# A fused RWKV-5 attention and cosine-router MoE kernel: drains on GpSimd, a branch hint, two loads swapped and two small tables moved

## The chip, the cores and the metric

The kernel runs on one core of a Trainium2 chip. The core has a matrix engine (TensorE, PE in the profile, with its weight loads as PEld), a vector engine (VectorE, DVE), an activation engine (ScalarE, ACT), a programmable engine (GpSimd, POOL) and an engine that mostly issues transfers (SyncE, SP). Each engine runs its own list of instructions in order, and they wait for one another by semaphores. The metric is the time on the device for one execution, in microseconds; a lower time is better. A profiled execution gives the trace that all views below are taken from.

## The reference, cut to what matters

Two computations follow each other. The first is a recurrence over 768 steps for 4 batches of 8 heads of 48 columns; the second sends each of the 3072 resulting rows to one of 8 experts.

```python
# attention: r, k, v are (4, 8, 768, 48); w and u are (8, 48)
for t in range(S):
    kt, vt, rt = k[:, :, t], v[:, :, t], r[:, :, t]
    cur = einsum('bhd,bhe->bhde', u[None] * kt, vt)
    y[:, :, t] = einsum('bhd,bhde->bhe', rt, state + cur)
    state = w[None, :, :, None] * state + einsum('bhd,bhe->bhde', kt, vt)
# x = y as 3072 rows of 384
logits = normed(x) @ normed(expert_emb).T / tau
expert_idx = argmax(logits); gate_w = softmax(logits)[expert_idx]
for e in range(8):                       # w1[e] is 384 x 1024, w2[e] is 1024 x 384
    h = maximum(x[mask] @ w1[e], 0.0)
    out[mask] = gate_w[mask, None] * (h @ w2[e])
```

All data are float32.

## The kernel before

**The attention** is cut into 24 units: 6 chunks of 128 steps by 4 batches. Unit i needs a K, an R and a V tile of 192 KB each; `load` issues the three, and the units are pipelined, five units ahead for the loads. For each unit GpSimd makes three products of 128x384: K times a power of the decay (`scaled`), K times u (`own_k`), and that times R (`own_r`). The last of them gives each step's own term, which VectorE sums to `diag` and ScalarE multiplies with V (`own_rows`).

```python
def load(k, i, K=None):
    ...
    nc.sync.dma_start(out=K, in_=of(k.k))
    R = k.Rpad[i % len(k.Rpad)]
    nc.sync.dma_start(out=R[:, :, 0:D], in_=of(k.r))
    V = k.io.tile([128, H, D], F32, name="V", tag="V")
    if i == 0:
        k.u_bc = ...                      # u, broadcast over the partitions
        nc.sync.dma_start(out=k.u_bc..., in_=...)
    nc.sync.dma_start(out=V, in_=of(k.v))
    k.loaded[i] = (K, R, V)

def scaled(k, i):
    k.nc.gpsimd.tensor_mul(k.Kpad[i % len(k.Kpad)][:, :, 0:D], k.loaded[i][0], k.kpow)
def own(k, i):
    own_k(k, i)
    own_r(k, i)
def own_k(k, i):
    k.KU[i] = ...
    k.nc.gpsimd.tensor_mul(k.KU[i], k.loaded[i][0], k.u_bc)
def own_r(k, i):
    k.nc.gpsimd.tensor_mul(k.KU[i], k.KU[i], k.loaded[i][1][:, :, 0:D])
```

`build_first` loads units 0 to 3 and calls `own_k(k, 0)`; the first turn of the loop (i = -1) then calls `scaled` for unit 1, `own_r` for unit 0 and `own` for unit 1, in this order.

**The tables** are small constants that the routing needs. `build_turned` is a generator: each `next(tables)` emits the VectorE instructions up to the next `yield`. The first three steps come in turns 1, 2 and 3, the last one in turn 9 (2 * B + 1 with B = 4).

```python
def build_turned(k):
    ...                                   # bits of a partition number, `own`, `mask`
    yield
    nc.vector.scalar_tensor_tensor(k.turned, k.qt, own[:, 1:2], k.turned, ALU.is_equal, ALU.mult)
    nc.vector.tensor_scalar_add(k.turned, k.turned, -1.0)      # both 128x64
    k.tie = pool.tile([128, E], F32, name="tie")
    nc.vector.tensor_scalar(k.tie, k.number, N + 1.0 / 16, None, ALU.mult)
    yield
```

**The experts** follow the attention, eight turns with the weights loaded ahead. In each turn GpSimd only issues indirect transfers: it gathers rows of x for an expert three turns ahead, and scatters the finished rows of this one to the output. Each of them is one DMA_INDIRECT of 128 rows or fewer; two more gathers stand in the attention's end. TensorE never stops in these turns.

```python
for i in range(E):
    doubled = blocks[i].weigh_out() if i > 0 else blocks[0].halves()
    for b in at(i + 1):
        b.hidden(doubled)
    do(doubled)
    if i == E - 1:
        blocks[i].rest()                  # rows past 256: scatters
    ready = [b.weigh() for b in at(i + 2)] + [b.halves() for b in at(i + 1)]
    blocks[i].out(itertools.chain(*ready))    # the first 256 rows: two scatters
    first_weights(i + 3)
    ...                                   # turn of i + 2, rest() of turns before the last
    for b in at(i + 3):
        b.gather()
    second_weights(i + 2)
```

**The general path** lies behind a branch at the end (`again`). It is for inputs that the quick path can't do (an expert with too many rows, decays out of range); with these inputs it is not entered, and every engine loads a flag and jumps over it.

```python
left = nc.values_load(flag[0:1, 0:1], min_val=0, max_val=1)   # L1458
with tc.If(left > 0):                                         # L1459
    ...                                                       # hundreds of instructions
```

Behind the branch each engine brings its semaphores to the values that the general path would have left, GpSimd does so for those of its own transfers with one INC_SWDGE_SEM, and a closing sequence with drains and barriers of all engines ends the program (L1602 in the profile).

Of the kernel before, what the change touches and what calls it, by code (L numbers as in the profile page):

```python
# [17 lines left out]
B, H, S, D = 4, 8, 768, 48  # L18
DM, E, F = H * D, 8, 1024
# [29 lines left out]
def build_first(k):  # L49


    nc, pool = k.nc, k.aconst
    wc = pool.tile([128, NP], F32, name="wc")
    nc.vector.memset(wc, 1.0)
    with nc.allow_non_contiguous_dma(reason="384 words"):
        for s, q in ((0, nc.sync), (1, nc.scalar)):
            q.dma_start(out=wc[s * DP : s * DP + D, :], in_=k.w.rearrange("(p s) d -> s d p", s=2)[s])
    k.ones = k.const.tile([128, 128], F32, name="ones")
    nc.vector.memset(k.ones, 1.0)
    wide = k.work.tile([128, 512], F32, name="wide", tag="AT1")  # L60
    nc.vector.memset(wide, 1.0)
    k.ident = k.const.tile([128, 128], F32, name="ident")
    make_identity(nc, k.ident)

    def busy(columns):
        ps = k.ps.tile([128, 512], F32, name="wake", tag="y")
        nc.tensor.matmul(ps[:, 0:columns], k.ones, wide[:, 0:columns], start=True, stop=True)

    for _ in range(WAKE):
        busy(512)  # L70
    k.Kpad, k.Rpad = (
        [pool.tile([128, H, DP], F32, name=f"{name}{i}") for i in range(count)]
        for name, count in (("Kpad", 4), ("Rpad", AHEAD + 2))
    )
    pads = k.Kpad + k.Rpad
    for t in pads:
        nc.gpsimd.memset(t[:, :, D:DP], 0.0)
    load(k, 0, k.Kpad[0])
    for i in range(1, AHEAD - 1):
        load(k, i)  # L80
    load_rows(k)


    nc.gpsimd.tensor_scalar(wc, wc, W_MIN, W_MAX, ALU.max, ALU.min)
    build_numbers(k)
    own_k(k, 0)
    t = pool.tile([128, NP, C], F32, name="wpow")
    for p in range(NP):
        nc.vector.tensor_tensor_scan(
            t[:, p, :], wc[:, p : p + 1].to_broadcast([128, C]), k.ones, 1.0, ALU.mult, ALU.mult  # L90
        )
    mid = pool.tile([128, NP], F32, name="mid")
    nc.vector.reciprocal(mid, t[:, :, C // 2])
    kp = k.work.tile([128, NP, C], F32, name="kp", tag="AT0")
    nc.vector.tensor_mul(kp, t[:, :, ::-1], mid[:, :, None].to_broadcast([128, NP, C]))
    k.rpow = pool.tile([128, NP, C], F32, name="rpow")
    for p in range(NP):
        nc.scalar.mul(k.rpow[:, p, :], t[:, p, :], mid[:, p : p + 1])
    cast(k)

    kt = turned_k(k, 0)
    k.KT[0] = k.work.tile([128, NP, C], F32, name="KT", tag="KT")
    nc.vector.tensor_mul(k.KT[0], kt, kp)
    turn_r(k, 0)
    ps = k.ps.tile([128, NP, 2, DP], F32, name="kpT", tag="xp")
    for p in range(NP):
        nc.tensor.transpose(ps[:, p].rearrange("q s d -> q (s d)"), kp[:, p, :], k.ident)
    busy(192)
    k.kpow = pool.tile([128, H, D], F32, name="kpow")
    nc.vector.tensor_copy(k.kpow.rearrange("q (p s) d -> q p s d", s=2), ps[:, :, :, 0:D])  # L110
    first = k.Kpad[0].rearrange("q (p s) d -> q p s d", s=2)[:, :, :, 0:D]
    nc.vector.tensor_mul(first, first, ps[:, :, :, 0:D])
    k.wC = t[:, :, C - 1 : C].to_broadcast([128, NP, D])
# [77 lines left out]
def build_turned(k):  # L191


    nc, pool = k.nc, k.const
    no_counts(k)
    bits = pool.tile([2 * QS, 3], I32, name="bits")
    nc.vector.tensor_scalar(bits[:, 0:1], k.part, 2, E - 1, ALU.arith_shift_right, ALU.bitwise_and)
    nc.vector.tensor_scalar(bits[:, 1:2], k.part, 3, None, ALU.bitwise_and)
    nc.vector.tensor_scalar(bits[:, 2:3], k.part, 3, 4, ALU.arith_shift_right, ALU.bitwise_and)
    yield  # L200
    own = pool.tile([2 * QS, 3], F32, name="own")
    nc.vector.tensor_copy(own, bits)
    nc.vector.tensor_add(own[:, 1:2], own[:, 1:2], own[:, 2:3])
    yield
    k.mask = pool.tile([2 * QS, E], F32, name="mask")
    nc.vector.tensor_scalar(k.mask, k.number, own[:, 0:1], None, ALU.is_equal)
    yield
    nc.vector.scalar_tensor_tensor(k.turned, k.qt, own[:, 1:2], k.turned, ALU.is_equal, ALU.mult)
    nc.vector.tensor_scalar_add(k.turned, k.turned, -1.0)

    k.tie = pool.tile([128, E], F32, name="tie")
    nc.vector.tensor_scalar(k.tie, k.number, N + 1.0 / 16, None, ALU.mult)
    yield
# [72 lines left out]
def load(k, i, K=None):  # L286

    nc = k.nc
    c, b = divmod(i, B)

    def of(src):
        return src[b, :, c * C : (c + 1) * C, :].rearrange("h s d -> s h d")

    K = k.io.tile([128, H, D], F32, name="K", tag="K") if K is None else K[:, :, 0:D]
    nc.sync.dma_start(out=K, in_=of(k.k))
    R = k.Rpad[i % len(k.Rpad)]
    nc.sync.dma_start(out=R[:, :, 0:D], in_=of(k.r))
    V = k.io.tile([128, H, D], F32, name="V", tag="V")
    if i == 0:
        k.u_bc = k.aconst.tile([128, H, D], F32, name="u_bc")  # L300
        nc.sync.dma_start(
            out=k.u_bc.rearrange("p h d -> p (h d)"),
            in_=bass.AP(tensor=k.u.tensor, offset=k.u.offset, ap=[[0, 128], [1, DM]]),
        )
    nc.sync.dma_start(out=V, in_=of(k.v))
    k.loaded[i] = (K, R, V)


def pair(t, p):
# [7 lines left out]
# [7 lines that stand above are left out]
    k.KU[i] = k.work.tile([128, H, D], F32, name="KU", tag="KU")  # L324
# [5 lines that stand above are left out]
# [8 lines left out]
def own_rows(k, i, half):  # L338
    if half == 0:
        k.xd[i] = k.work.tile([128, H, D], F32, name="xd", tag="xd")  # L340
    diag, V = k.diag[i], k.loaded[i][2]
    for h in range(half * H // 2, (half + 1) * H // 2):
        k.nc.scalar.mul(k.xd[i][:, h, :], V[:, h, :], diag[:, h : h + 1])  # L343

# [499 lines left out]
def attention(k):  # L844
# [16 lines left out]
    emb, tables = build_experts(k), build_turned(k)  # L861
    for i in range(-1, units):
# [16 lines left out]
        if i == B + 3:  # L879
            norms(k, k.groups[0])  # L880
        on(scaled, i + 2)
        if i < 0:
            own_r(k, 0)
        on(own, i + 2)
        for n in SQUARES.get(i, (i - 1,)):
            of_group(squares, n)
# [28 lines left out]
        whole(taken, i - 6, "xp")  # L915
        whole(exps, i - 4)
        on(carry, i)
        if i in (1, 2, 3):
            next(tables)
        whole(summed, i - 6)  # L920
        on(scores, i + 1)
# [16 lines left out]
            build_constants(k)  # L938
        if i in (1, 2, 3):
            next(emb)  # L940
        if i == 2 * B + 1:
            next(tables)
        if 3 <= i < 3 + len(k.ring):
            k.nc.gpsimd.memset(k.ring[i - 3], 0.0)
        if j == 8:
# [426 lines left out]
def experts(k):  # L1372

    blocks = [Block(k, r) for r in TURN]
    for b, (w1, w2) in zip(blocks, k.weights):
        b.w1, b.w2 = w1, w2

    def at(i):
        return [blocks[i]] if i < E else []

    def first_weights(i):
        for b in at(i):
            b.w1 = w1_tile(k)
            load_w1(k, expert_number(k, b.rank), b.w1)

    def second_weights(i):
        for b in at(i):
            b.w2 = w2_tile(k)
            load_w2(k, expert_number(k, b.rank), b.w2)

    for b in blocks[0:2]:
        b.gather()
        b.turn()
    do(blocks[1].Tx)
    do(blocks[1].weigh())
    do(blocks[0].weigh_out())
    blocks[0].plain()
    first_weights(2)
    blocks[2].gather()
# [4 lines that stand above are left out]
        do(doubled)  # L1404
        if i == E - 1:
            blocks[i].rest()
        ready = [b.weigh() for b in at(i + 2)] + [b.halves() for b in at(i + 1)]
        blocks[i].out(itertools.chain(*ready))
        first_weights(i + 3)
        for b in at(i + 2):  # L1410
            b.turn()
            do(b.Tx)
        if 256 < blocks[i].n and i < E - 1:
            blocks[i].rest()
            if i == 2:
                decays(k)
        for b in at(i + 3):
            b.gather()
        second_weights(i + 2)


# [26 lines left out]
def again(k):  # L1448


    nc, tc, need = k.nc, k.tc, k.need
# [4 lines left out]
    nc.vector.tensor_copy(flag[:, 0:1], some)  # L1456
    nc.vector.tensor_copy(flag[:, 1:2], k.far)
    left = nc.values_load(flag[0:1, 0:1], min_val=0, max_val=1)  # L1458
    with tc.If(left > 0):  # L1459
        nc.sync.dma_start(out=k.need_dram.rearrange("e g -> (e g)").unsqueeze(0), in_=as_int(k, need))  # L1460
        far = nc.values_load(flag[0:1, 1:2], min_val=0, max_val=1)
        with tc.If(far > 0):
            no_counts(k)
            recur(k)
            with ExitStack() as ctx:
                attention_pools(k, ctx)
                for c in range(NCH):
# [4 lines left out]
                    out=k.need_dram.rearrange("e g -> (e g)").unsqueeze(0), in_=as_int(k, grouped(k, count))  # L1472
# [134 lines left out]
```

## Time and profile before

The time is 406.03 us (median of 3 runs, 405.99 to 406.11). The profiled execution has a span of 403.8 us.

| stage, us from the span's start | what runs | PE busy in it |
|---|---|---|
| 0 to 131 | attention and routing, 24 units | 22.43 of the first 25, 34.58 of the next 35, 70.01 of the next 71 |
| 131 to 160 | last routing, two early expert tiles | 28.64 of 29 |
| 160 to 385 | eight experts | 225.00 of 225 |
| 385 to 404 | last scatters, branch, closing sequence | 6.73 of 19 |

Over the whole span PE is busy for 387.4 us (96%), VectorE for 254.3 (63%), ScalarE for 172.6 (43%) and GpSimd for 161.1 (40%). Such a table is read by asking for each stage which engine's waits end last. Where PE is full, moving the work of another engine changes nothing unless PE waits for it; where no engine is busy, in the last stage, the time lies in transfers and in instructions that the busy columns leave out. In the group and timeline views a row shows the engine, the line of the source, the operation, the tile written and the tiles read, and the time; a bracket behind a row tells how long the engine stood idle before it and what released it. A "q" behind an engine's name (POOLq) stands for instructions that only its sequencer carries out: branches, semaphore waits, drains.

### The profile page before, as it was taken

To read this page: it belongs to the slowest core of one execution; us is meant where nothing else is said; L and a number is where in the kernel's file an instruction comes from. 1 tells how busy PE (TensorE), PEld (TensorE's weight loads), DVE (VectorE), ACT (ScalarE), POOL (GpSimd) and SP (SyncE) were. 2 spreads that over 40 slices of the span, in tenths; PEclk is the share of its full clock that TensorE was granted. 3 is DMA by queue.
4 is the path that set the end of the run, shared out by engine and by line. 5 is a ranking of instruction groups with operands and counts; after the bars stand their busy time and mean duration, and the time that the engine had idled before them with its cause. 6 is when DMAs were issued, how large, how long until landed. Compare 5 with 4: busy or idle time off the path is not lost.

```text
span 403.8 us, 9257 instructions
## 1 busy us (share of the span) xinstructions
PE 387.4 (96%) x3542; PEld 352.9 (87%) x3542; DVE 254.3 (63%) x601; ACT 172.6 (43%) x523; POOL 161.1 (40%) x216
## 2 busy tenths in 40 slices
PE   7999999999999999999999999999999999999980
PEld 4988888888888877899999999999999999799670
DVE  6886888787788650677668666367267257466210
ACT  3888776777676413333333332232233233232110
POOL 7998795858663242301503202402321330300120
PEclk9999999999999999999999999999999999999995
DMA  8999777767616961246527341613524440420110
GB/s 156 192 221 220 156 155 146 155 137 152 130 41 211 335 233 38 85 159 210 199 67 248 95 157 39 223 41 153 174 83 156 136 140 2 134 82 1 58 40 26
DMA packets 93801, 54.39 MB, mean 135 GB/s; under 512 B 76938, under 2 KB 88381, under 8 KB 93747
## 3 DMA queue, kind: packets, MB, share of 16 engines
q1 hardware_dynamic: 90242, 44.26, 41.3%
q0 software_dynamic: 3296, 9.44, 7.3%
q8 instruction: 30, 0.49, 0.5%
q14 instruction: 25, 0.20, 0.2%
q10 hardware_dynamic: 208, 0.00, 0.0%
HBM read 44.45 MB, written 9.63 MB: 134 GB/s over the span
## 4 chain that ended last, share of the span: by engine, by line
PE 83%; ACT 3%; issue 3%; POOL 3%; DVE 2%; DMA 2%; SPq 1%; POOLq 0%; ACTq 0%
PE ps L1223 25%; PE ps L1287 16%; PE ps L1327 5%; PE at L385 4%; PE y L449 4%; PE ps L1341 4%; PE early_h L1033 3%; PE early_y L1042 3%; PE ps L1201 3%; PE yrows L467 3%; PE ps L1171 2%; PE y L440 2%; PE rt L357 2%; PE kt L366 2%; PE xp L553 2%
## 5 line engine op out<-in xcount | busy, mean ns | idle before, releaser
L1087 POOL DMA_INDIRECT out_dram<-y,to x25 | 30.2, 1206 | 173.5 <-issue 116.7
L1223 PE MATMUL ps<-xTe,w 128*128 128x192 f32 (+3 forms) x336 | 62.9, 327 | 0.0
L1223 PEld LDWEIGHTS ps<-xTe,w 128*128 128x128 f32 x336 | 55.9, 190 | 0.5
L343 ACT ACTIVATE xd<-V,diag 128x48 f32<-128x48 f32 x184 | 46.2, 325 | 0.0
L391 DVE TENSOR_TENSOR AT<-at,umask 128x512 f32<-128x512 f32 x48 | 32.7, 685 | 10.8 <-PE at L385 10.7
L1230 ACT ACTIVATE hT<-hT 128x384 f32<-128x384 f32 (+3 forms) x42 | 22.0, 523 | 32.4 <-DVE hT L1253 19.7
L1287 PE MATMUL ps<-Tw,Sh 128*128 128x192 f32 x192 | 32.5, 326 | 0.0
L1287 PEld LDWEIGHTS ps<-Tw,Sh 128*128 128x128 f32 x192 | 31.4, 190 | 0.0
L1078 POOL DMA_INDIRECT G<-xs,take x25 | 27.0, 1079 | 10.5 <-issue 4.0
L1223 PE MATMUL ps<-Tx,Sw 128*128 128x192 f32 (+3 forms) x168 | 29.6, 326 | 0.0
L385 PE MATMUL at<-RT,KT 48*128 48x128 f32 x384 | 27.9, 285 | 0.2 <-DVE RT L359 0.2
L1223 PEld LDWEIGHTS ps<-Tx,Sw 128*128 128x128 f32 x168 | 27.6, 190 | 0.1
L1240 DVE TENSOR_TENSOR u<-ps,p 128x384 f32<-128x384 f32 (+3 forms) x14 | 7.8, 558 | 31.0 <-ACT p L1237 16.3
L449 PE MATMUL y<-AT,V 128*48 128x128 f32 (+1 forms) x384 | 26.0, 277 | 0.0
L385 PEld LDWEIGHTS at<-RT,KT 48*128 48x128 f32 x384 | 23.3, 187 | 2.5 <-issue 0.9
L329 POOL TENSOR_TENSOR KU<-KU,Rpad 128x384 f32<-128x384 f32 x24 | 24.2, 1007 | 1.8
L314 POOL TENSOR_TENSOR Kpad<-K,kpow 128x384 f32<-128x384 f32 x23 | 23.2, 1008 | 0.9 <-DMA K<-in_k_dram 0.8
L449 PEld LDWEIGHTS y<-AT,V 128*48 128x48 f32 (+1 forms) x384 | 19.9, 124 | 4.1 <-issue 3.8
L1287 PE MATMUL ps<-w,hT 128*128 128x192 f32 x128 | 23.4, 326 | 0.0
L325 POOL TENSOR_TENSOR KU<-K,u_bc 128x384 f32<-128x384 f32 x23 | 23.3, 1012 | 0.0
L555 ACT COPY xT<-xp 128x384 f32<-128x384 f32 x24 | 11.5, 480 | 25.4 <-PE xp L553 25.4
L1250 ACT ACTIVATE hT<-ps 128x384 f32<-128x384 f32 (+3 forms) x14 | 6.9, 491 | 35.7 <-PE ps L1223 35.7
(240 smaller groups left out, 818.5 us busy)
## 6 DMA issues: line engine op xcount, KB each, us to landing
w<-in_moe_w_dram SPq DMA_DIRECT2D x16, 1536.0 KB, 7.4
Rpad<-in_r_dram SPq DMA_DIRECT2D x24, 192.0 KB, 3.9
V<-in_v_dram SPq DMA_DIRECT2D x24, 192.0 KB, 4.2
xs<-X SPq DMA_DIRECT2D x24, 192.0 KB, 2.6
K<-in_k_dram SPq DMA_DIRECT2D x23, 192.0 KB, 3.3
G<-xs,take POOLq DMA_INDIRECT x27, 3.2
out_dram<-y,to POOLq DMA_INDIRECT x25, 3.6
Kpad<-in_k_dram SPq DMA_DIRECT2D x1, 192.0 KB, 3.4
```

What stands on the lines that cost most here:

```text
L314: k.nc.gpsimd.tensor_mul(k.Kpad[i % len(k.Kpad)][:, :, 0:D], k.loaded[i][0], k.kpow)
L325: k.nc.gpsimd.tensor_mul(k.KU[i], k.loaded[i][0], k.u_bc)
L329: k.nc.gpsimd.tensor_mul(k.KU[i], k.KU[i], k.loaded[i][1][:, :, 0:D])
L343: k.nc.scalar.mul(k.xd[i][:, h, :], V[:, h, :], diag[:, h : h + 1])
L385: nc.tensor.matmul(at[s][:, p, :], KT[rows, p, :], RT[rows, p, :], start=True, stop=True)
L391: k.nc.vector.tensor_mul(a, k.at[i][s], k.umask[:, None, :].to_broadcast([128, NP, C]))
L449: mm(y[s][u * DP : u * DP + n, q, :], V[:, h * D : h * D + n], AT[s][:, p, :], start=(c == 0 and q == 0), stop=True, skip_group_check=True,)
L1078: nc.gpsimd.indirect_dma_start(out=G[0:n, :], out_offset=None, in_=k.xs[:, :], in_offset=IndirectOffsetOnAxis(ap=take[0:n], axis=0), bound ...
L1087: put = k.nc.gpsimd.indirect_dma_start(out=k.out[:, :], out_offset=IndirectOffsetOnAxis(ap=to, axis=0), in_=y, in_offset=None, bounds_chec ...
L1223: nc.tensor.matmul(ps[:, j, :], weights[:, (f + j) * 128 : (f + j + 1) * 128], moving, start=(first and j == 0), stop=True, skip_group_che ...
L1230: nc.scalar.activation(h, h, ACT.Relu)
L1287: nc.tensor.matmul(ps, a[:, f, :], b[:, f, :], start=(first and f == 0), stop=(f == NF // 2 - 1), skip_group_check=True)
```

## The change

Four edits, which do not touch each other.

1. **Drains.** A drain instruction is added on GpSimd at the end of each of the experts' turns 0 to 6, behind the gathers, and in turn 7 between the scatters of `rest()` and the two last ones. It has no semaphore to wait for or to set. That makes eight in all. They are meant to let GpSimd settle its transfers while TensorE works.
2. **A hint for the branch.** PE, DVE, ACT and POOL are told that the jump over the general path is likely. The call stands ahead of the experts; in the built program the hint is the first instruction of each of these four engines, behind the opening barrier.
3. **First V behind second K and R.** V of unit 0 is issued after K and R of unit 1, directly ahead of V of unit 1. With it `own_r` of unit 0 moves ahead of `scaled` of unit 1 on GpSimd. No transfer and no product is added.
4. **Tables in turns 1 to 5.** A `yield` between the two 128x64 operations splits the last step in two, and the five steps are taken in turns 1 to 5; nothing is left in turn 9.

```diff
     build_numbers(k)
-    own_k(k, 0)
+    own(k, 0)
@@ build_turned
     nc.vector.scalar_tensor_tensor(k.turned, k.qt, own[:, 1:2], k.turned, ALU.is_equal, ALU.mult)
+    yield
     nc.vector.tensor_scalar_add(k.turned, k.turned, -1.0)
@@ load
     V = k.io.tile([128, H, D], F32, name="V", tag="V")
+    k.loaded[i] = (K, R, V)
     ...
-    nc.sync.dma_start(out=V, in_=of(k.v))
-    k.loaded[i] = (K, R, V)
+    for n in () if i == 0 else (0, 1) if i == 1 else (i,):
+        nc.sync.dma_start(out=k.loaded[n][2], in_=of(k.v, n % B))
@@ attention, in the loop
-        if i < 0:
-            own_r(k, 0)
...
-        if i in (1, 2, 3):
+        if 0 < i < B + 2:
             next(tables)
...
-        if i == 2 * B + 1:
-            next(tables)
@@ experts
+    k.tc.mark_branch_hint_location(
+        "left", "LikelyTaken", engines=[... ("PE", "DVE", "Activation", "Pool")]
+    )
     for b in blocks[0:2]:
...
         if i == E - 1:
             blocks[i].rest()
+            k.nc.gpsimd.drain()
...
         for b in at(i + 3):
             b.gather()
+        if i < E - 1:
+            k.nc.gpsimd.drain()
         second_weights(i + 2)
@@ again
-    with tc.If(left > 0):
+    with tc.If(left > 0, label="left"):
```

More of the change, by code (lines that the diff above doesn't have):

```diff
@@ L289, in load, with of @@
     c, b = divmod(i, B)
-    def of(src):
+    def of(src, b=b):
         return src[b, :, c * C : (c + 1) * C, :].rearrange("h s d -> s h d")
@@ L1389, in second_weights @@
             load_w2(k, expert_number(k, b.rank), b.w2)
+    k.tc.mark_branch_hint_location(
+        "left", "LikelyTaken", engines=[getattr(mybir.EngineType, e) for e in ("PE", "DVE", "Activation", "Pool")]
+    )
     for b in blocks[0:2]:
```

## The prediction

> **What bounds the kernel now.** I read the page first: busy times, then the chain of waits.
>
> ```profile
> PE 387.4 (96%) x3542; PEld 352.9 (87%) x3542; DVE 254.3 (63%) x601; ACT 172.6 (43%) x523; POOL 161.1 (40%) x216
> PE 83%; ACT 3%; issue 3%; POOL 3%; DVE 2%; DMA 2%; SPq 1%; POOLq 0%; ACTq 0%
> ```
>
> PE carries 83% of the chain, and the table by stage shows it full from 160 to 385 us. No part of the change adds or removes a matmul, so in 225 of 404 us nothing can be gained. What is left is the head (0 to 25 us), the attention where VectorE delays PE, and the tail behind 385 us. Each of the four edits aims at one of these. I looked at the tail first, because there all busy columns are almost empty. Its instructions run on the sequencers, so I asked for the source lines of the branch (L1459) and of the closing sequence (L1602); the columns are duration in ns (min/median/max) and first and last start in us.
>
> ```profile
> L1459 POOLq EVENT_SEMAPHORE  x6: 17/30/43, 396.7 to 397.1; - x6
> L1459 POOLq COMPARE_BRANCH  x1: 61/61/61, 392.8 to 392.8; - x1
> L1459 POOLq INC_SWDGE_SEM  x1: 1260/1260/1260, 397.2 to 397.2; - x1
> ...
> L1602 SPq EVENT_SEMAPHORE  x14: 17/28/28, 398.4 to 403.7; - x14
> ...
> L1602 POOLq DRAIN  x3: 46/107/4482, 398.5 to 403.5; - x3
> ...
> L1602 SPq DRAIN  x3: 7/7/13, 399.2 to 403.2; - x3
> ```
>
> GpSimd branches at 392.8 and starts its next instruction at 396.7. It then sets its transfers' semaphores (1.26 us from 397.2) and drains for 4.48 us from 398.5 to 403.0. SyncE is done with its own semaphores at 399.2 and waits for that drain; two barriers then take 0.75 us.
>
> The head is a GpSimd matter; this is its timeline (start, duration, idle time before with its releaser):
>
> ```profile
> 6.52 1.01 POOL L325 TENSOR_TENSOR KU<-Kpad,u_bc 128x384 f32<-128x384 f32 x1 [1.06 <-DMA u_bc<-in_u_dram]
> 8.33 1.00 POOL L314 TENSOR_TENSOR Kpad<-K,kpow 128x384 f32<-128x384 f32 x1 [0.80 <-DMA K<-in_k_dram]
> 9.29 1.01 POOL L329 TENSOR_TENSOR KU<-KU,Rpad 128x384 f32<-128x384 f32 x1
> ```
>
> GpSimd stands idle for 0.80 us, from 7.53 to 8.33, for K of unit 1, although `own_r` of unit 0 has all it needs. From 8.33 it is nearly continuously busy (21.56 of the first 25 us), so lost time here is passed on.
>
> The tables show in the middle, in turn 9:
>
> ```profile
> 59.62 1.01 POOL L325 TENSOR_TENSOR KU<-K,u_bc 128x384 f32<-128x384 f32 x1
> ...
> 59.74 0.97 DVE L208 SCALAR_TENSOR_TENSOR turned<-qt,own,turned 128x64 f32<-128x64 f32 x1
> ...
> 60.72 1.01 POOL L329 TENSOR_TENSOR KU<-KU,Rpad 128x384 f32<-128x384 f32 x1
> ...
> 60.75 1.02 DVE L209 TENSOR_SCALAR turned<-turned 128x64 f32<-128x64 f32 x1
> ```
>
> Each 128x64 operation on VectorE ends when the GpSimd product beside it ends. The same size of TENSOR_SCALAR (L796) takes 0.25 us elsewhere.
>
> **What the Trainium skill says.** "SBUF — State Buffer", section "SBUF: two separate sides", calls the port pair of VectorE and GpSimd an exclusive lock: whichever starts first holds it for its whole instruction. The lines above agree (1.02 beside GpSimd, 0.25 without). "Runtime: NRT & Kernel Launch", section "Instruction fetch mechanics", says that a taken branch to a page that isn't loaded stalls for a fetch; the 3.8 us behind GpSimd's branch fit. "Perfetto Trace Analysis", section "Sequencer-only Instruction (DRAIN, etc)", puts the recorded start of a drain after its semaphore waits, so the 4.48 us are its own execution. What that execution depends on, no page states.
>
> **The change, part by part.**
>
> *Drains.* Added: eight on GpSimd. In the experts' turns GpSimd issues 25 scatters and 25 gathers of about 1 us each and stands idle some 15 to 21 us before each turn's first scatter, so a drain at the turn's end lies beside PE's work. The last one follows the scatter that ends at 384.55 and the next scatter starts at 391.66: even 4.5 us fit there. Cost on the path: 0. The gain depends on what the last drain does in 4.48 us. The drain at the program's start, with no transfer behind it, takes 0.19 us. If the long one settles all 54 indirect transfers, that is (4.48 - 0.19) / 54 = 0.08 us for each; after the change two are left, and it should take 0.19 + 2 x 0.08 = 0.35 us. It would then end at 398.5 + 0.35 = 398.85, earlier than SyncE's last drain at 399.23, so SyncE takes over, and I count not 4.1 but 402.98 - 399.24 = **3.7 us**. If instead the time belongs to the semaphore instruction ahead of it, or is fixed, the gain is 0.
>
> *Hint.* Four instructions, some tenths of a us at the start at most. On PE, ACT and VectorE the fetch is off the path. On GpSimd 3.8 us could go, but the next thing it does is to wait for the last scatter, and the trace's landing records put that one's last packet at 396.54 (4.0 us from issue to landing in the view of DMA issues, as the median of the last two). With two waits' spacing behind it the semaphore instruction could start at about 396.85 and not 397.21: **0.35 us**. The transfer hides the rest.
>
> *First V, and own_r.* K of unit 1 is issued at 3.62 and R at 4.45; they move ahead of V (3.14). `own_r` then fills the hole: it runs 7.53 to 8.53, `scaled` of unit 1 follows at 8.53 (0.20 later than now, and K should have landed), and all from `own_k` of unit 1 (10.25 now) comes at 9.53, 0.7 us earlier. PE gets R earlier too (it waits 0.74 us for it at 9.50) and V, landing where R landed before, near 9.4, still comes before its first use at 10.49. PE's own path gains less than GpSimd: the transposed K of unit 1 moves from 9.96 to 9.55, so unit 1 gains 0.4. I choose **0.45 us**, between 0.4 and 0.7.
>
> *Tables.* The score matmuls (L385) start every 5.48 and 5.60 us in the like places of the two later chunks (85.11 to 90.59 and 106.70 to 112.30), and 6.21 us behind turn 9 (62.79 to 69.00). Turn 9 thus loses about 0.65 us of the 2.0 that VectorE spends. In turns 4 and 5 the two operations land in a VectorE gap of 0.7 us (idle before 31.14 and 36.22), where ScalarE is the bound. One may be held by GpSimd, as the 128x8 mask of turn 3 is now (1.64 us); I take 0.15 us off: **0.5 us**.
>
> The sum with the drain working: 3.7 + 0.35 + 0.45 + 0.5 = 5.0, so 401.0 us. Without it: 1.3, so 404.7 us.
>
> **Rivals.** *The drain is fixed or belongs to the semaphore instruction.* For it: that instruction stands directly ahead of it and does much more than at the start (1.26 us against 0.03). Against it: nothing else on GpSimd is outstanding except the transfers, and the start's pair of the same two instructions is short. It makes 404.7. *In-turn drains hold gathers or scatters.* A drain could wait for the landing of transfers (2.5 to 7.1 us in the scatters' source view). Still it ends before the next turn's scatter; only if each took over 15 us would PE wait. It would make 408 or more; I give it 3 in 100. *The hint, so far ahead of its branch, does nothing, or fetches a page at the start that delays the first instructions.* The first is 0.35 lost, the second up to a fetch of 3.8 us, which would eat the gains: 5 in 100. *V late.* If V of unit 0 lands after 10.1, the first unit's product waits for it and the head gains nothing.
>
> **Range and chances.** I give the short last drain 65 in 100 and the unchanged one 35. The weighted time is 0.65 x 401.0 + 0.35 x 404.7 = 402.3; I lean to the likelier side and say 402.0. The range must hold both: from 400.2 (all parts at their full size, hint included) to 405.4 (no drain gain, half of the small parts). A gain over 2% needs 8.1 us, more than all parts together; a loss over 2% needs a stall that no view suggests. I give 0.02 to each.
>
> **What would show it.** The last GpSimd drain at L1602: under 0.5 us if I am right, 4.5 if the rival is. SyncE's last drain should be what the barrier waits for. In-turn drains: short, and PE's busy time from 160 to 385 still 225 us. GpSimd's first semaphore wait behind the branch should start within 0.5 us of it, with the landing at 396.5 less the shift as the new end. At the head: no GpSimd idle time before `scaled` at 8.5, and score matmuls of unit 1 near 11.5 and not 11.96. The two `turned` operations stand near 30 and 35 us, and the interval behind turn 9 falls to about 5.5. What would make it wrong: a last drain of a third length, or head gains that vanish at the next shared wait.

## The result, and the profile after

The kernel after takes 399.5 us (median of 6 runs, 399.23 to 399.93) where the kernel before takes 406.1 us (405.99 to 406.52). The ratio is 0.9837, with a 95% interval of 0.9824 to 0.985: 6.6 us less, and not the 4.0 that was predicted. The time lies below the predicted range. The profiled spans are 403.8 and 397.8 us.

First the page of the kernel after: busy times, then the chain of waits.

```profile
PE 387.8 (97%) x3542; PEld 352.7 (89%) x3542; DVE 254.5 (64%) x601; ACT 172.6 (43%) x523; POOL 161.9 (41%) x216
PE 91%; ACT 3%; DVE 1%; POOL 1%; DMA 1%; issue 1%; SPq 0%; POOLq 0%; DVEq 0%
```

The work is the same, and PE's share of the chain rises from 83 to 91%: what went away was no work of any engine. The tail shows it. These are the source lines of the scatters (L1086), the branch (now L1466) and the closing sequence (L1609), with durations in ns (min/median/max) and the first and last start in us. Two lines of the kernel before stand first, the scatters and PE's branch.

```profile
L1087 POOL DMA_INDIRECT out_dram<-y,to x25: 883/978/1906, 189.8 to 392.9; - x25
...
L1459 PEldq COMPARE_BRANCH  x1: 3602/3602/3602, 389.3 to 389.3; - x1
```

```profile
L1086 POOL DMA_INDIRECT out_dram<-y,to x25: 883/981/1902, 189.7 to 392.8; - x25
```

```profile
L1466 POOLq EVENT_SEMAPHORE  x6: 17/30/43, 393.2 to 395.9; - x6
...
L1466 PEldq COMPARE_BRANCH  x1: 396/396/396, 389.1 to 389.1; - x1
...
L1466 POOLq COMPARE_BRANCH  x1: 72/72/72, 392.7 to 392.7; - x1
L1466 POOLq INC_SWDGE_SEM  x1: 240/240/240, 396.0 to 396.0; - x1
```

```profile
L1609 SPq EVENT_SEMAPHORE  x14: 17/28/28, 396.2 to 397.7; - x14
...
L1609 POOLq DRAIN  x3: 46/109/213, 396.2 to 397.5; - x3
L1609 SPq DRAIN  x3: 7/7/13, 396.9 to 397.2; - x3
```

Read against the lines of before: the last drain takes 0.213 us and not 4.482; the semaphore instruction ahead of it takes 0.240 and not 1.260; GpSimd's first wait behind the branch starts at 393.2 and not at 396.7. The scatter that these waits are for starts 0.14 us earlier than before (392.80, before 392.94), but the landing records put its last packet at 395.69, where before it was 396.54: 2.89 us from the start of its instruction and not 3.60. A scatter leaves 16 landing records. Thirteen of the 16 come at the same distance in both (2.43 to 2.58 us before, 2.40 to 2.55 after); the last three come at 3.27, 3.43 and 3.60 us before and at 2.58, 2.79 and 2.89 after. What the first closing barrier waits for is now SyncE's drain at 396.97, as GpSimd's ends at 396.46.

At the head GpSimd's timeline has no idle time left between the products:

```profile
6.78 1.00 POOL L328 TENSOR_TENSOR KU<-Kpad,u_bc 128x384 f32<-128x384 f32 x1 [1.19 <-DMA u_bc<-in_u_dram]
7.86 1.00 POOL L332 TENSOR_TENSOR KU<-KU,Rpad 128x384 f32<-128x384 f32 x1
8.82 1.00 POOL L317 TENSOR_TENSOR Kpad<-K,kpow 128x384 f32<-128x384 f32 x1
```

Still `scaled` (the third row) starts at 8.82, later than before (8.33), and the score matmuls of unit 1 at 11.93 (before 11.96). The tables stand in turns 4 and 5; this is VectorE's timeline, with one row of GpSimd's:

```profile
29.99 1.00 POOL L332 TENSOR_TENSOR KU<-KU,Rpad 128x384 f32<-128x384 f32 x1
...
30.30 0.77 DVE L208 SCALAR_TENSOR_TENSOR turned<-qt,own,turned 128x64 f32<-128x64 f32 x1
...
35.39 0.19 DVE L210 TENSOR_SCALAR turned<-turned 128x64 f32<-128x64 f32 x1
```

They cost 0.96 us of VectorE and not 1.99. The first of them is still beside a GpSimd product and again ends 0.08 us behind it; it is the second, with GpSimd idle when it starts, that became short. And the interval between the score matmuls behind turn 9 falls from 6.21 to 5.47 us (62.77 to 68.24).

### The profile page after: what moved, and what is told of

It reads as the page before. It is cut to its first block, busy times and chain, and to the rows that moved or that the text cites. A ratio compares the mean times of both kernels' runs of the same rounds, so it can differ in the third digit from the quotient of the medians.

```text
span 397.8 us, 9267 instructions
## 1 busy us (share of the span) xinstructions
PE 387.8 (97%) x3542; PEld 352.7 (89%) x3542; DVE 254.5 (64%) x601; ACT 172.6 (43%) x523; POOL 161.9 (41%) x216
## 3 DMA queue, kind: packets, MB, share of 16 engines
q0 software_dynamic: 3296, 9.44, 7.4%
## 4 chain that ended last, share of the span: by engine, by line
PE 91%; ACT 3%; DVE 1%; POOL 1%; DMA 1%; issue 1%; SPq 0%; POOLq 0%; DVEq 0%
PE ps L1222 25%; PE ps L1286 18%; PE ps L1326 5%; PE at L388 5%; PE y L452 5%; PE ps L1340 4%; PE yrows L470 3%; PE early_h L1032 3%; PE early_y L1041 3%; PE ps L1200 3%; PE rt L360 2%; PE ps L1170 2%; PE y L443 2%; PE kt L369 2%; PE st L409 2%; PE xp L556 2%
## 5 line engine op out<-in xcount | busy, mean ns | idle before, releaser
L1086 POOL DMA_INDIRECT out_dram<-y,to x25 | 29.7, 1187 | 172.7 <-DVE Sh L1361 108.7
L1077 POOL DMA_INDIRECT G<-xs,take x25 | 28.2, 1130 | 10.5 <-issue 5.8
L558 ACT COPY xT<-xp 128x384 f32<-128x384 f32 x24 | 11.5, 478 | 25.1 <-PE xp L556 23.9
```

Source lines behind the costliest of these rows:

```text
L1077: nc.gpsimd.indirect_dma_start(out=G[0:n, :], out_offset=None, in_=k.xs[:, :], in_offset=IndirectOffsetOnAxis(ap=take[0:n], axis=0), bound ...
L1086: put = k.nc.gpsimd.indirect_dma_start(out=k.out[:, :], out_offset=IndirectOffsetOnAxis(ap=to, axis=0), in_=y, in_offset=None, bounds_chec ...
```

## The experiments

### Each part by itself

Four kernels, each the kernel before with one of the four edits of the diff, on one chip, where before took 406.05 us.

**Drains alone** (`+ k.nc.gpsimd.drain()` at the end of turns 0 to 6 and in turn 7).

> The kernel before with the eight drains alone. Theory A (drains settle the transfers, per transfer): last drain 0.2 us and semaphore instruction 0.24 us as with all four parts, GpSimd still starts behind its branch at about 396.6 us for want of the hint, SyncE becomes the last to reach the barrier; 4.8 us faster than before, 401.3 us. Theory B (the drains also make the last scatter land earlier, by clearing what stands before it): the last scatter lands 2.9 us after its start and not 3.6, but the branch's fetch still holds GpSimd, so the same time; the landing tells B from A. Theory C (the hint matters for the drain): last drain stays at several us, time near 405.

Measured: 401.2 us, ratio 0.9878 (0.9863 to 0.9893), 4.85 us less. The semaphore instruction takes 0.235 us and the last drain 0.209; the scatter still lands 3.37 us from its start.

```profile
L1462 POOLq INC_SWDGE_SEM  x1: 235/235/235, 397.5 to 397.5; - x1
L1605 POOLq DRAIN  x3: 46/107/209, 397.7 to 399.0; - x3
```

**The hint alone** (`+ k.tc.mark_branch_hint_location("left", "LikelyTaken", engines=[PE, DVE, Activation, Pool])`, and the label on the branch).

> The kernel before with the hint alone. Theory A (the fetches of the four engines at the branch share the 16 transfer engines with the last scatters and delay them, and the hint takes them away): last scatter lands about 2.9 us after its start and not 3.6, the semaphore instruction starts at about 396.1 us (397.2 before) but still takes 1.26 us, and the last drain still 4.5 us: 1.0 us faster, 405.1 us. Theory B (the earlier landing belongs to the drains): landing 3.6 us after its start as before, gain 0.35 us, 405.7 us. My prediction's own step said 0.35 us.

Measured: 405.16 us, ratio 0.9979 (0.9971 to 0.9987), 0.89 us less. The source lines of its branch:

```profile
L1462 POOLq EVENT_SEMAPHORE  x6: 17/30/43, 393.5 to 396.2; - x6
...
L1462 POOLq INC_SWDGE_SEM  x1: 1272/1272/1272, 396.3 to 396.3; - x1
```

The last scatter starts at 393.14 here, so the last of GpSimd's waits comes about 3.1 us behind it (before 397.1 - 392.9 = 4.2). Without drains the semaphore instruction stays long, as before. The hint thus doesn't only let GpSimd wait sooner: the transfer itself is over sooner. What it costs is about 0.1 us at the start: the first load of K is issued at 1.46 us and not at 1.36.

**The tables alone** (`+ yield`, and `if 0 < i < B + 2: next(tables)` in place of turns 1 to 3 and 9).

> The kernel before with the tables in turns 1 to 5 alone. Theory A (a gain in the attention reaches the end): the interval behind turn 9 falls from 6.21 to 5.47 us, and the time falls by 0.75 us to 405.35. Theory B (what is won is lost again between 126 and 160 us, as the trace of the changed kernel shows 0.76 us at 120 us and 0.15 us at 160 us): time falls by 0.15 us to 405.95.

Measured: 405.11 us, ratio 0.9977 (0.9967 to 0.9986), 0.94 us less. The interval behind turn 9 is 5.47 us (63.31 to 68.78); the trace accounts for 0.74 of the 0.94.

**V and `own_r` alone** (the order of the loads, and `own(k, 0)` in `build_first`).

> The kernel before with V of unit 0 behind K and R of unit 1 and own_r of unit 0 ahead of scaled of unit 1, nothing else. My prediction's step said 0.45 us. The trace of the changed kernel says that score matmuls of unit 1 start 0.03 us earlier, so theory B: no gain, 406.1 us within 0.1, because own_r ahead of scaled holds the transpose of K that PE waits for, while GpSimd's own lead of 0.5 us is not waited for by anybody.

Measured: 406.61 us, ratio 1.0007 (0.9998 to 1.0015). No gain (the interval reaches from 0.1 us less to 0.6 us more). The four differences add up to -4.85 - 0.89 - 0.94 + 0.56 (or about 0.3 by the ratio) = -6.1 to -6.4, against the -6.6 of all four: the parts are nearly independent.

### What the last drain's length depends on

Four kernels with one drain only, at the end of turn 0, 2, 4 or 6, so that 36, 23, 9 or 3 indirect transfers come behind it. One edit, with n = 0, 2, 4, 6:

```diff
         for b in at(i + 3):
             b.gather()
+        if i == n:
+            k.nc.gpsimd.drain()
```

> The kernel before with one drain only, at the end of turn 0: 18 indirect transfers lie ahead of it, 36 behind. Read are the semaphore instruction and the last drain on GpSimd, together 5.74 us with 54 transfers behind and 0.44 us with 2. Theory A (each transfer that no drain has settled costs the same): 0.24 + 36 x 0.102 = 3.9 us together. Theory B (a list of limited length, full well below 54): 5.7 us as without any drain. Theory C (the number of drains counts, not their place): a little under 5.7 us.

> The kernel before with one drain only, at the end of turn 2: 31 indirect transfers ahead, 23 behind. Theory A (same cost per unsettled transfer): 0.24 + 23 x 0.102 = 2.6 us for the semaphore instruction and the last drain together. Theory B (limited list): 5.7 us, or a lower value if the list is shorter than 23. Theory C (number of drains): the same as with the drain in turn 0.

> The kernel before with one drain only, at the end of turn 4: 45 indirect transfers ahead, 9 behind. Theory A: 0.24 + 9 x 0.102 = 1.2 us for the semaphore instruction and the last drain together. Theory C: the same as with the drain in turn 0. The drain itself should take the settling of 45 transfers (4.6 us) plus the wait until its last gather has landed, some 8 to 9 us from its start, and still end before the next scatter.

> The kernel before with one drain only, at the end of turn 6: 51 indirect transfers ahead, 3 behind. Theory A: 0.24 + 3 x 0.102 = 0.55 us for the semaphore instruction and the last drain together, so nearly all of what eight drains give. The scatter behind it could start at 383.57 at the earliest and the drain begins near 378, so if it takes over 5.5 us it delays that scatter, but not the last two.

The source lines of the branch (L1461) and the closing sequence (L1604), in the order turn 0, turn 2, turn 4, turn 6:

```profile
L1461 POOLq INC_SWDGE_SEM  x1: 900/900/900, 399.5 to 399.5; - x1
L1604 POOLq DRAIN  x3: 46/107/2998, 400.4 to 403.9; - x3
```

```profile
L1461 POOLq INC_SWDGE_SEM  x1: 640/640/640, 399.7 to 399.7; - x1
L1604 POOLq DRAIN  x3: 46/107/1937, 400.4 to 402.9; - x3
```

```profile
L1461 POOLq INC_SWDGE_SEM  x1: 368/368/368, 399.4 to 399.4; - x1
L1604 POOLq DRAIN  x3: 46/107/788, 399.8 to 401.1; - x3
```

```profile
L1461 POOLq INC_SWDGE_SEM  x1: 248/248/248, 397.8 to 397.8; - x1
L1604 POOLq DRAIN  x3: 46/107/298, 398.1 to 399.3; - x3
```

The numbers to read are the duration of the first line and the maximum of the second. With the two ends, the kernel before and the kernel after, they make a straight line:

| transfers behind the last in-turn drain | semaphore instruction, us | last drain, us | sum | line 0.25 + 0.102 n |
|---|---|---|---|---|
| 54 (before) | 1.260 | 4.482 | 5.74 | 5.76 |
| 36 | 0.900 | 2.998 | 3.90 | 3.92 |
| 23 | 0.640 | 1.937 | 2.58 | 2.60 |
| 9 | 0.368 | 0.788 | 1.16 | 1.17 |
| 3 | 0.248 | 0.298 | 0.55 | 0.56 |
| 2 (after) | 0.240 | 0.213 | 0.45 | 0.45 |

So the time is neither fixed nor a matter of how many drains there are: it is 0.102 us for each indirect transfer since the last drain, some 0.02 of it in the semaphore instruction and 0.08 in the drain. The count fits better than the bytes. The transfers behind the drain move 9.44, 6.31, 4.11, 1.73, 0.58 and 0.39 MB in the order of the table; a straight line through the two ends of the table misses the sums between them by at most 0.013 us when it is drawn over the count, and by up to 0.08 us when it is drawn over the MB.

The settling shows in the added drains as well. With 18, 31, 45 and 51 transfers ahead of it, the one drain ends 1.07, 1.77, 2.22 and 3.15 us behind the last packet of these transfers. The times of these executions were 406.2, 404.92, 403.47 and 401.61 us (before 406.42 in the same group), one execution each, and only their tails are used.

### V and `own_r` taken apart, and one drain in place of eight

Four kernels on one chip, where before took 407.26 us (406.58 to 409.38): all four parts again as a control; the same without the edit of the loads; with V moved, but `own_r` of unit 0 left behind `scaled` of unit 1; and all four with only the drain of turn 7. Against the kernel after:

```diff
# without the loads: V and own_r as in the kernel before
# V alone:
-    own(k, 0)
+    own_k(k, 0)
@@ in the loop, behind scaled
+        if i < 0:
+            own_r(k, 0)
# one drain:
-        if i < E - 1:
-            k.nc.gpsimd.drain()
```

> All four parts, the same instructions as the kernel after, as the control of this group. Expected: 399.5 us, ratio to before 0.984. Last two GpSimd instructions (setting the semaphores 0.24, last drain 0.21 us). Unit 1's score matmuls at 11.9 to 12.3 us.

> Drains, hint and tables, loads and own_r as before. Theory A (moving V and own_r together gives nothing): 399.4 to 399.7 us, within 0.3 of the control, unit 1 at 11.9 to 12.1 us. Theory B (the part is worth its predicted 0.45 us but was spoiled by chance in its own run): 399.95 us, 0.45 above the control.

> As the control, with V of unit 0 behind K and R of unit 1, but own_r of unit 0 left behind scaled of unit 1, as in the kernel before. Theory A (K of unit 1 lands earlier and scaled, and behind it the transposed K of unit 1, follow it; own_r ahead of it takes 1.0 us of GpSimd from this): scaled of unit 1 starts near 7.9, its transposes near 9.5, unit 1 near 11.5, time 399.1 us, 0.4 below the control. Theory B (the landing of R and V sets unit 1, not K): unit 1 at 11.9 to 12.3, time within 0.2 of the control.

> As the control, but only the drain in turn 7, between the scatters of the last rows past 256 and the last two scatters; the other seven are left out. Theory A (one drain settles whatever stands behind it, some 0.08 us each, once the last of it has landed): this drain takes about 2.9 + 50 x 0.08 = 6.9 us from 383.4, ends at 390.3, ahead of the next scatter at 391.7, so 399.5 us as the control, with the last two instructions at 0.24 and 0.21 us. Theory B (the drains of the turns before are needed, or the settling costs 0.1 us each and more): it ends past 391.7, holds the last scatters, and the time is 400 to 402 us.

| | time, us | ratio to before (95%) | `scaled` behind the start of `own_k` | unit 1's score matmuls |
|---|---|---|---|---|
| all four | 401.02 (400.67 to 402.73) | 0.9849 (0.982 to 0.9877) | 9.92 - 7.88 = 2.04 | 13.03 |
| without the loads | 400.9 (400.64 to 403.15) | 0.9849 (0.9819 to 0.988) | 9.74 - 8.14 = 1.60 | 13.29 |
| V alone | 400.11 (399.95 to 400.28) | 0.982 (0.9795 to 0.9845) | 8.86 - 7.89 = 0.97 | 12.03 |
| one drain | 401.69 (400.62 to 402.96) | 0.9855 (0.9824 to 0.9885) | 9.88 - 7.84 = 2.04 | (lower clock) |

GpSimd's timelines of the head say why. With all four parts:

```profile
7.88 1.00 POOL L327 TENSOR_TENSOR KU<-Kpad,u_bc 128x384 f32<-128x384 f32 x1 [2.32 <-DMA u_bc<-in_u_dram]
8.96 1.00 POOL L331 TENSOR_TENSOR KU<-KU,Rpad 128x384 f32<-128x384 f32 x1
9.92 1.00 POOL L316 TENSOR_TENSOR Kpad<-K,kpow 128x384 f32<-128x384 f32 x1
```

Without the edit of the loads (the bracket names VectorE, but what came late is K of unit 1, as in the profile of before):

```profile
8.14 1.00 POOL L326 TENSOR_TENSOR KU<-Kpad,u_bc 128x384 f32<-128x384 f32 x1 [2.56 <-DMA u_bc<-in_u_dram]
9.74 1.00 POOL L315 TENSOR_TENSOR Kpad<-K,kpow 128x384 f32<-128x384 f32 x1 [0.61 <-DVE Kpad L112]
```

With V alone moved:

```profile
7.89 1.00 POOL L327 TENSOR_TENSOR KU<-Kpad,u_bc 128x384 f32<-128x384 f32 x1 [2.35 <-DMA u_bc<-in_u_dram]
8.86 1.00 POOL L316 TENSOR_TENSOR Kpad<-K,kpow 128x384 f32<-128x384 f32 x1
```

With V out of the way `scaled` follows `own_k` with no wait at all. Moving V closes the hole by itself; `own_r` ahead of `scaled` then fills nothing, it takes 1.07 us of GpSimd from the product that PE waits for. PE's transposes of unit 1 begin at 9.92 with V alone and at 10.97 with both. When u arrives changes from execution to execution (`own_k` starts at 6.5 to 8.1 us in these profiles), so the distances from `own_k` are compared. With both moved, `scaled` comes 2.04 us behind it also in the kernel after and in the kernel with the loads alone (9.22 - 7.18); with the loads as before it is 1.55 to 1.81, set by the landing of K (9.61 us without the edit of the loads, 0.13 ahead of `scaled`). Unit 1's score matmuls follow `own_k` by 5.15 us with both moved, by 5.11 to 5.44 with the loads as before, and by 4.06 to 4.14 with V alone (all at the full clock in this stretch). The time agrees: all runs with V alone lie below all runs of the control, by 0.9 us in the median, though the ratios' intervals overlap. It is more than the 0.4 us that was expected.

One drain is enough. Its median is 0.7 us above the control's, with ratios of 0.9855 and 0.9849 whose intervals nearly coincide, so no difference is shown. In some executions, the profiled one with one drain among them, TensorE's granted clock is 0.5 for 3.4 us from about 12 us on, and what follows comes about 2 us later; without the executions whose mean granted clock was 0.992 or less (three of six with one drain, one of six of the control) the times are 400.62 to 401.05 and 400.67 to 401.11 us. The last two instructions take 0.240 and 0.217 us, as with eight drains, and the single drain itself takes this long:

```profile
L1408 POOLq DRAIN  x1: 5535/5535/5535, 386.1 to 386.1; - x1
```

It ends at 391.59 and the next scatter starts at 394.39, so it holds nothing up. With eight drains, and so one transfer ahead of it in place of 52, that same drain takes 2.857 us. The 51 more transfers cost 2.68 us here, 0.05 each and not the 0.08 that had been expected (6.9 us); part of the settling may run while the drain waits for the last landing, which is not shown.

### Where the tables' gain went in the kernel after, and whose fetches slow the scatter

In the kernels with single parts the stretch from the score matmuls of the last attention unit to the first main matmul of the experts takes 43.25 us, as before. In the kernel after it takes 43.86 and in the four of the last group 43.60 to 43.85, which gives back up to 0.6 of the tables' 0.74. A pair of parts seemed to make it. Four more kernels, on one chip (before 406.92): before with hint and tables; before with drains and tables; V alone with the hint on GpSimd only; and V alone once more as the control.

```diff
# hint on GpSimd only:
-        "left", "LikelyTaken", engines=[... ("PE", "DVE", "Activation", "Pool")]
+        "left", "LikelyTaken", engines=[... ("Pool",)]
```

> The kernel before with the hint and the tables, no drains, loads as before. Read is the stretch from the score matmuls of the last unit to the first main matmul of the experts. Theory A (hint and tables together give back what the tables gain): 43.6 to 43.9 us. Theory B (drains and tables do it): 43.25. Theory C (all three are needed): 43.25 in all three pairs.

> The kernel before with the drains and the tables. The same stretch: theory A 43.25 us, theory B 43.6 to 43.9, theory C 43.25.

> As the version with V alone moved, the drains and the tables, but the hint on GpSimd alone. Theory A (a hint on PE or ScalarE, with the tables, makes the stretch 43.8): 43.25 us here, 0.5 us gained. The last scatter: if the fetches of PE, ScalarE and VectorE slow it, its landing takes 3.4 to 3.6 us from the start of its instruction and not 2.9, so 0.6 is lost and the time is that of the control, within 0.3 us; if GpSimd's own fetch slowed it, it stays at 2.9 and the time is 0.5 below the control.

> The version with V of unit 0 behind K and R of unit 1, own_r behind scaled, with drains, hint and tables; control of this group. Expected: ratio to before 0.981 to 0.984, so 398.5 to 399.5 us where before takes 406.1; the stretch 43.85 us, last scatter 2.9 us.

The stretch is 43.25 us in all four, and so in the control, the very kernel that had shown 43.85 in the group before. The theory of a pair fell: the stretch differs between executions of one kernel. What makes it 0.6 us longer in some is open; ScalarE's second copy of a unit's `y` starts 0.52 us late there, although the records of the matmuls that it waits for stand in the same places.

The times were 400.43 us with the hint on GpSimd only (ratio 0.9819, 0.9782 to 0.9857) and 399.45 us for the control (0.9803, 0.9766 to 0.9841). The two pairs, run once each for the stretch, took 406.63 and 403.01 us. The tail of the kernel with the hint on GpSimd only:

```profile
L1465 POOLq EVENT_SEMAPHORE  x6: 17/30/43, 392.9 to 396.7; - x6
...
L1465 PEldq COMPARE_BRANCH  x1: 3322/3322/3322, 388.8 to 388.8; - x1
...
L1465 POOLq COMPARE_BRANCH  x1: 72/72/72, 392.4 to 392.4; - x1
```

And of the control, with the hint on four engines:

```profile
L1465 POOLq EVENT_SEMAPHORE  x6: 17/30/43, 392.8 to 395.4; - x6
...
L1465 PEldq COMPARE_BRANCH  x1: 393/393/393, 388.7 to 388.7; - x1
```

In both GpSimd goes on 0.52 us behind its branch. But its last wait stands at 396.7 in the first and at 395.4 in the second, with the last scatter at 392.52 and 392.43: 4.2 us against 3.0. So about 1.2 us of landing in this pair depend on the hints of the *other* engines (0.6 had been expected), and the medians of the time lie 0.98 us apart. GpSimd's own hint adds nothing that these profiles show (4.2 in the kernel before as well). The DMA records show the traffic: with the hint on GpSimd only, five instruction fetches (8 to 16 KB) start between 392.5 and 396.3, one of them of 16 KB in 1.77 us at 392.94, while the scatter is under way; with four hints there are two of 8 KB, at 393.45 and 393.46. Over all profiles of this study the same holds: from the start of the last scatter to the start of GpSimd's semaphore instruction it is 3.09 to 3.19 us in the eight kernels with four hints, and 3.75 to 4.30 in the ten others. How a fetch delays the scatter is not shown. That only the last few of a scatter's 16 landing records come late would fit fetches that stand in its way on some of the transfer engines.

## Why the prediction was wrong, point by point

**Drains, predicted 3.7, measured 4.85.** The mechanism was right: the last drain settles what has been issued, 0.08 us each, and eight drains leave 0.21 us. The step that failed is the sum's last one, that SyncE's last drain at 399.23 takes over as a fixed end, so that only 3.7 of the drain's 4.1 us count. SyncE does take over, but its end moves: its own semaphore row starts when GpSimd's semaphore instruction ends (398.4 before, 396.2 after), and that instruction shrinks by 1.02 us. With it 3.74 + 1.02 = 4.76 of the 4.85 are found. The prediction had set the drain's settling against a cost of the semaphore instruction; in truth the two instructions share one cost of 0.102 us for each transfer. The 35 in 100 for no gain moved the forecast 1 us further off, to 402.0, and the lower end of the range, 400.2, left out what the semaphore instruction and the landing could give.

**The drains in the turns** are not short, as I said they would be: 4.73 to 7.57 us in turns 0 to 6, by the first of these lines. Their records start while GpSimd is still issuing the transfers ahead of them (in turn 0 from 193.36, with the last of these instructions ending at 198.30), and they end behind the landing: the one in turn 7, with one transfer ahead of it, at 386.21, its scatter's last packet at 386.13. The 4.48 us of the last drain in the kernel before hold no such wait, because the last landing (396.54) lies ahead of its start (398.5).

```profile
L1425 POOLq DRAIN  x7: 4729/7073/7570, 193.4 to 378.0; - x7
```

```profile
L1410 POOLq DRAIN  x1: 2845/2845/2845, 383.4 to 383.4; - x1
```

They cost nothing, because they lie in GpSimd's idle time before each turn's first scatter: PE is still busy for 225.00 us from 160 to 385, as in the profile of before.

**The hint, predicted 0.35, measured 0.89.** GpSimd's first wait came 0.52 us behind its branch, as predicted. The fetch stall that the Trainium skill tells of ("Runtime: NRT & Kernel Launch", section "Instruction fetch mechanics") is gone from the trace on all four engines (PE's branch 3.6 us before, 0.4 after). The step that failed is "on PE, ACT and VectorE the fetch is off the path". Their waits are off the path, but the last scatter lands later when they fetch at the branch, and I had taken its landing at 396.54 as given. It was the landing that moved, from 3.60 to about 2.9 us behind the scatter's start.

**Tables, predicted 0.5, measured 0.94 alone.** The interval behind turn 9 is 5.47 us, as predicted 5.5. Two terms were mis-sized: turn 9 gave 0.74 us and not 0.65, and the 0.15 us that I took off for turns 4 and 5 wasn't spent. One of the two operations did run beside a GpSimd product again (0.77 us), but the intervals of these turns are 5.42 and 5.08 us in both kernels. Of the 0.94, the other 0.2 is within the interval of the ratio.

**V and `own_r`, predicted 0.45, measured none.** Unit 1's score matmuls stand at 11.93 and not near 11.5. The step that failed is that `own_r` "fills the hole". I moved K ahead, which removes the hole, and counted on the hole as well: with K there `scaled` could start 0.97 us behind `own_k`, and the edit lets it start at 2.04. The transposed K of unit 1, which was to come at 9.55, came at 9.88. (0.26 us of that miss is u, which let `own_k` start at 6.78 and not at 6.52.) GpSimd's later products did come sooner, by 0.5 us of the 0.7 predicted (`own_k` of unit 1 at 9.78, before 10.25), which was useless, because PE waits for `scaled`. V was not late: the first product with V starts at 10.46, before 10.49.

**The sum.** 4.85 + 0.89 + 0.94 + 0 = 6.7, against 6.6 measured. That they meet so closely is partly luck: each term has an interval of some tenths, and the profile of the kernel after loses 0.6 us in the stretch ahead of the experts. Predicted with the drains working: 5.0. Of the 1.7 missing, 1.15 are the drains' term, 0.54 the hint's and 0.44 the tables', less 0.45 for the loads.

## What to carry to other kernels

Where a program ends on the engine that issued many indirect transfers, look for the semaphore instruction and the drain at its end, divide their time by the transfers, and put one drain into an idle stretch ahead of the last transfers; here one was enough. A hint for a branch that jumps over much code is worth trying on all engines and not only on the one on the path: here the end waited for a scatter, which landed sooner when the others didn't fetch. When two edits cure the same wait, try each alone: here the version with V moved and `own_r` left in place took 400.11 us on the chip where all four parts took 401.02, and 399.45 on another.

## What the runs showed of the hardware that was not expected

- A drain on GpSimd ends behind the landing of the indirect transfers issued ahead of it (0.08 us behind it with one, 2.75 with 52), and at the program's end both it and the semaphore instruction grow with the number of transfers since the last drain: together 0.102 us for each, from 0.45 us with 2 to 5.74 us with 54.
- With the branch hint missing on PE, ScalarE and VectorE, five instruction fetches and not two started while GpSimd's last scatter was under way, and GpSimd's last wait came 4.2 us and not 3.0 behind the scatter's start.
- A 128x64 operation on VectorE with one input took 1.02 us beside a GpSimd product and 0.19 us with GpSimd idle at its start. The one with two inputs took 0.97 and 0.77 us, both times until 0.08 us behind the end of the product beside it.
- One kernel's stretch between attention and experts took 43.25 us in one execution and 43.85 in another, at a granted clock of 1.00 in both; the cause is open.
